# A list-scheduled attention and two-FFN kernel: longer transfer reserves in its planner, a wait narrowed to one PSUM bank, and a third token tile transposed by TensorE

## The chip, the cores and the metric

One core of one Trainium2 chip runs the whole program in one launch. The metric is device time in microseconds, the median of several runs. A difference under 0.3% (2 us here) can't be told from no change.

## The reference

For 4 sequences of 576 tokens, 8 heads of width 64, a windowed causal attention (64 keys back) is followed by two feed-forward layers over all 2304 tokens:

```python
scores = where((rel >= 0) & (rel < 64), q @ k.T / 8, -1e9)
x = softmax(scores) @ v                    # 2304 x 512
h = relu(x @ w_in); x = (h * h) @ w_out    # 512 -> 2048 -> 512
h = x @ w2_in                              # 512 -> 1024
solu = h * softmax(h)
out = layernorm(solu) * g_ln @ w2_out      # 1024 -> 512
```

## The kernel before

Each float32 product is made of three products (`TERMS`) of operands that were split into a high and a low part in a 32-bit matmul type. ScalarE (ACT) rounds the high part, VectorE (DVE) subtracts for the low one.

The order of all work is set before the program is built. Every piece is a task of `Plan`: an engine, a length in us, a rank, the tasks it comes after, buffer slots it takes and gives, and `late`, a time added behind its end before others may start. For a DMA `late` stands for the transfer, and the length for issuing it on SP's queue. `Plan.run` repeatedly starts the task that can start first (ties by rank), and the instructions are emitted in the order of the planned starts. On the chip each engine runs its own list in order and waits for the true dependencies by semaphores; nothing is reordered there. So a number in the plan changes no instruction, only its place.

Stages, in the order of time:

- **Stage one** (to about 140 us). Attention units of two 64-token blocks, 18 in all, run beside the first FFN for the first tokens (products of 256 and 512 columns: lines L693 for FFN1's first matmul, L709 for its second). A unit is: load q, k (`load_qk`) and v, scores on PE (L423), a mask and a maximum on DVE (L426, L431), exponentials on ACT (L448), a normalization (L458), a transpose, the product with v (`values`, L516 or L519), and for later tokens a store to DRAM (`store_x`). In the first ten units PE transposes (L476). PE fills its first 48 us with idle-time matmuls (`ps_warm`).
- **Stage two** (140 to about 257 us). The first FFN for the next 768 tokens, in eight rounds (`pair1`, t = 2) of seven half-size products each, 384 columns (L919), with the second matmul's products (L1036) between them. The last eight units run beside it. They are "crossed": DVE transposes 32x32 blocks (L482, `d`), a DMA writes them to DRAM (`aside`, L485), four DMAs read them back across partitions (`across`, L490, `pt`), and only then PE may run `values` (L516).
- **Stage three** (to about 434 us): the same FFN for the last 1024 tokens, 512 columns.
- **Stage four** (`pair2`, from about 434 us): the second FFN, nine pairs of 128-token tiles. A pair has seven products of six matmuls (L1314), in the order p1, p6, p7, p5, p2, p4, p3, into four banks a, b, d, c, of 512 columns: p1 and p2 go to a, p6 to b, p7 and p4 to d, p5 and p3 to c. `keep1` (ACT, L1320) copies p1 out of a; `u2`, `u3`, `c22`, `c21`, `c12` (DVE) and `c11` (ACT) add and copy banks. Then `behind` does softmax and layernorm for each tile: L1387 to L1406. The tile must be transposed for the last matmul (`mm_o`, L1455, 24 matmuls a tile). For the first 16 tiles DVE transposes blocks (L1415) and two DMA steps turn them through DRAM (L1418, L1424); for the last two (`TURNED`) PE transposes them, 8 matmuls each (L1438, `ps_lt`). `scaled` (ACT, L1460) and a store end a tile.

Of the kernel before, what the change touches and what calls it, by code (L numbers as in the profile page):

```python
# [20 lines left out]
P = 128  # L21
# [77 lines left out]
def kernel(  # L99
# [20 lines left out]
    NT, DM = out.shape  # L120
    DC = DM // P
    KF = w_in.shape[0]
# [6 lines left out]
    PASSES = [8, 0, 12, 16]  # L129
# [62 lines left out]
    with ExitStack() as c1:  # L192
# [7 lines left out]
        pass_of, starts = {}, []  # L200
# [8 lines left out]
        add = plan.add  # L209
# [134 lines left out]
        def attention(n, rank, after=()):  # L344
# [196 lines left out]
            if n == 0:  # L541
                lqs = [add("SP", 1.1, rank - 6, lambda h=h: load_qk(h), take=qk * (h == 0), late=2.0, at=0.7) for h in range(2)]
            else:
                lqs = [add("SP", 2.1 if alone else 2.2, rank - 6, lambda: load_qk(0), take=qk, late=2.0, at=0.7)]
            lv = add("SP", 0.9 if alone else 1.5, rank + (V0 if alone else -2), load_v, [v_after.get(n - 1) if n != 1 else None, *after], take=[vs], late=2.0, at=0.7)
            v_after[n] = lv
# [44 lines left out]
            else:  # L591
# [6 lines left out]
                if crossed:  # L598
                    c = add("DVE", 1.2, rank, blocks, ns, take=["raw"], give=["e"], port=True)
                    c = add("SP", 0.8, rank, aside, [c], late=LATE_P, give=["raw"])  # L600
                    c = [add("SP", 1.6, rank, across, [c, before], take=["pt"], late=LATE_P)]
                else:
                    c = [add("ACT", 0.48, rank, lambda a=a: copied(a), [p[a]], give=["a" if begins else "t"]) for a in range(2)]
                p = add("PE", 1.15, rank, lambda: values(0), [*c, lv], take=["t"], give=["pt", vs])
                if t < 2:
                    h = add("ACT", 0.48, rank, lambda: high(0), [p])
                    x_ready[n] = add("DVE", 0.60, rank, lambda: rest(0), [h], give=["t"])
                else:
                    h = add("ACT", 0.48, rank, taken, [p], take=["wm"], give=["t"])
                    x_ready[n] = add("SP", 0.8, rank, store_x, [h], late=2.8, give=["wm"])  # L610
            p_after[n] = p
# [72 lines left out]
        def ffn(n0, n1, kk, rank, done):  # L684
# [29 lines left out]
            if kk >= PUT:  # L714
# [10 lines left out]
                return  # L725
            r = add("ACT", N / 1200 + 0.11, rank, relu, [i], take=["r"], give=["a"])
            e = squares_of(o, N, rank, [r], signed=False)
# [167 lines left out]
        def pair1(t, j, at, unit, held, begins_after=()):  # L895
            N = HN[t]
# [3 lines left out]
            def rank(k):  # L900
                return at + unit * k
# [54 lines left out]
            def store(x, kk):  # L956
                nc.sync.dma_start(out=r_dram[t][kk], in_=o[x])
# [36 lines left out]
            for x, kk, f, k in (("c22", 2 * j + 1, f22, 6), ("u3", 2 * j, f21, 7)):  # L994
                f = squared(Named({}, o, x), N, rank(k) + 3, [f], False, True)
                r_ready[t, kk] = add("SP", 0.8, rank(k) + 3, lambda x=x, kk=kk: store(x, kk), [f], late=2.2, give=["wm"])

# [112 lines left out]
        PAIR0, PAIR = 10.88, 8.6  # L1110
        LATE, LATE_X, LATE_P, TOPS = 2.8, 4.0, 3.2, KF
        JOIN, SECOND, MORE = 4, 0.17, PASSES[1]
        SKIP = 6 if MORE else KF
# [40 lines left out]
        for t in (2, 3):  # L1154
# [13 lines left out]
            if t == 2:  # L1168
                lo, hi = begin[2] + 4, begin[3] - ENDS
                for i in range(PASSES[3] // 2):  # L1170
                    attention(starts[3] // 2 + i, lo + i * (hi - lo) / (PASSES[3] // 2), [xop[2, x][0] for x in ("S1", "S3", "S2", "S4")] if i < 2 else [])
                for m in range(NH2 * DC):
# [85 lines left out]
        def pair2(n, rank, rank_o):  # L1258
# [85 lines left out]
            def c12():  # L1344
# [3 lines left out]
            a = add("SP", 1.6, lead - 6, load_x, [x for _, t, at in tiles for x in stored[t, at * BLK // HN[t]]] + phase_of.get(n - 2, []) + [first_of[LAST, KF // 2 - 1] if n == 0 else past[LAST][-1], ready["2o", KF2 - 1] if n else None],  # L1348
                    take=["raw"], late=2.2)
            s1 = add("DVE", 0.72, lead, s13, [a], take=["raw"], port=True)  # L1350
# [9 lines left out]
            soon = rank - 30  # L1360
            free = read_of.get(n - 1, [])
            p1 = pe(0, "a", "A11", "B11", True, free if n > 1 else [], take=["a"] if n < 2 else ["b"] * (n == 2))
            e1 = add("ACT", 0.60, soon, keep1, [p1, *gone_by, *free])
            p6 = pe(1, "b", "S2", "T2", True, [p1, *free], take=["b"] * (n == 0))
            e2 = add("DVE", 0.68, soon, u2, [p6, e1, *gone_by, *free])
            p7 = pe(2, "d", "S3", "T3", True, [p6, *free], take=["a"] * (n < 2))
            p5 = pe(3, "c", "S1", "T1", True, [p7])
            e3 = add("DVE", 0.68, soon, u3, [p7, e2], take=["wm"])
# [6 lines left out]
            f12 = add("DVE", 0.68, soon, c12, [p3, f11, f21])  # L1375
            phase_of[n], read_of[n] = [p3], [f11, f12, f21]

# [3 lines left out]
        def behind(k, i, p, rank, rank_o, done):  # L1381
# [29 lines left out]

            by_pe = i >= NT // P - TURNED

# [59 lines left out]
            else:  # L1473
                p_ = add("DVE", 1.2, rank, blocks2, [a], port=True)
                r = add("ACT", 1.25, rank + 3, squares, [p_])
                p_ = add("SP", 0.8, rank, aside, [p_], late=2.4, give=["wb"])
                p_ = add("SP", 1.6, rank, across, [p_], take=["g"], late=2.4)
                r = add("POOL", 2.0, rank, root, [r], give=["wb"])
# [10 lines left out]

        EARLY0, LATE0, TURNED = 20, 20, 2  # L1490
        l_free = {(k, hf): past[LAST] for k in range(2) for hf in range(2)}
# [64 lines left out]
```

## Time and profile before

| | us |
|---|---|
| median of 3 runs | 651.33 (650.02 to 651.84) |
| the profiled execution | 651.62 |
| its span, first to last instruction | 649.8 |
| PE busy | 635.9 |
| DVE busy | 501.3 |
| ACT busy | 385.8 |
| POOL busy | 130.9 |

The span and busy times are of one profiled execution; its own time has 1.8 us around the span. PE's busy time includes overlap of pipelined matmuls, so it tells where PE is idle, not how close it is to its peak. L numbers are lines of the kernel before.

### The profile page before, as it was taken

To read this page: it belongs to the slowest core of one execution; us is meant where nothing else is said; L and a number is where in the kernel's file an instruction comes from. 1 tells how busy PE (TensorE), PEld (TensorE's weight loads), DVE (VectorE), ACT (ScalarE), POOL (GpSimd) and SP (SyncE) were. 2 spreads that over 40 slices of the span, in tenths; PEclk is the share of its full clock that TensorE was granted. 3 is DMA by queue.
4 is the path that set the end of the run, shared out by engine and by line. 5 is a ranking of instruction groups with operands and counts; after the bars stand their busy time and mean duration, and the time that the engine had idled before them with its cause. 6 is when DMAs were issued, how large, how long until landed. Compare 5 with 4: busy or idle time off the path is not lost.

```text
span 649.8 us, 11333 instructions
## 1 busy us (share of the span) xinstructions
PE 635.9 (98%) x4089; PEld 536.6 (83%) x4089; DVE 501.3 (77%) x872; ACT 385.8 (59%) x879; POOL 130.9 (20%) x164
## 2 busy tenths in 40 slices
PE   8999999999899999999999999999999999999997
PEld 4788877888889999998888888888887878878886
DVE  6998999599999663398887774499787798788761
ACT  5757757457767644466564554564755667557662
POOL 1012103123445433003333333100100110011000
PEclk9999999999999999999999999999999999999999
DMA  8887777215789667735431115742524643565311
GB/s 283 276 286 256 256 261 249 90 46 174 229 266 313 193 219 224 262 131 195 148 128 65 66 65 162 250 132 74 205 104 113 195 138 115 137 195 161 116 48 65
DMA packets 71353, 111.90 MB, mean 172 GB/s; under 512 B 6400, under 2 KB 42752, under 8 KB 71296
## 3 DMA queue, kind: packets, MB, share of 16 engines
q1 hardware_dynamic: 70752, 110.90, 52.5%
q8 instruction: 32, 0.52, 0.3%
q10 hardware_dynamic: 544, 0.26, 0.1%
q14 instruction: 25, 0.20, 0.1%
HBM read 76.01 MB, written 35.13 MB: 171 GB/s over the span
## 4 chain that ended last, share of the span: by engine, by line
PE 62%; DVE 5%; DMA 4%; ACT 3%; SPq 2%; issue 1%; ACTq 0%; DVEq 0%
PE ps_y L1036 22%; PE ps_h L919 17%; PE ps_o L1455 12%; PE ps_h L1314 10%; DMA l<-t_dram 1%; PE ps_v L516 1%; DMA pt<-p_dram 1%; SPq L1424 1%; DVE e L1398 1%; DMA p_dram<-d 1%; ACT o L1460 1%; ACT e L1406 1%; ACT e L448 1%; DVE wo L872 1%; DVE lnT L1448 1%
## 5 line engine op out<-in xcount | busy, mean ns | idle before, releaser
L1036 PE MATMUL ps_y<-g,wb 128*128 128x384 f32 (+1 forms) x768 | 163.7, 362 | 0.7 <-DVE g L642 0.7
L1036 PEld LDWEIGHTS ps_y<-g,wb 128*128 128x128 f32 x768 | 138.8, 188 | 16.7 <-DVE g L642 1.1
L1455 PE MATMUL ps_o<-w2o,lnT 128*128 128x512 f32 x432 | 100.4, 390 | 0.2 <-DVE lnT L1448 0.2
L1455 PEld LDWEIGHTS ps_o<-w2o,lnT 128*128 128x128 f32 x432 | 80.7, 188 | 17.8 <-DVE lnT L1448 0.5
L627 POOL TENSOR_TENSOR r<-r 128x512 f32<-128x512 f32 (+2 forms) x36 | 39.0, 1086 | 194.6 <-ACT r L699 116.8
L642 DVE TENSOR_TENSOR g<-r,g 128x512 fp32r<-128x512 f32 (+2 forms) x68 | 42.6, 627 | 28.1 <-ACT g L639 27.5
L627 POOL TENSOR_TENSOR u<-u 128x384 f32<-128x384 f32 (+1 forms) x48 | 47.9, 1003 | 77.9 <-ACT u L624 45.3
L1314 PE MATMUL ps_h<-w2i,xx 128*128 128x512 f32 x243 | 62.6, 390 | 0.0
L639 ACT ACTIVATE g<-r 128x512 fp32r<-128x512 f32 (+2 forms) x68 | 38.3, 566 | 33.7 <-PE ps_y L1036 16.9
L1314 PEld LDWEIGHTS ps_h<-w2i,xx 128*128 128x128 f32 x243 | 45.5, 188 | 9.8 <-DVE u L1324 0.3
L919 PE MATMUL ps_h<-xa,wo 128*128 128x512 f32 (+1 forms) x192 | 51.6, 368 | 0.0
L448 ACT ACTIVATE e<-e,nmax 128x128 f32<-128x128 f32 x112 | 43.5, 392 | 11.0 <-DVE nmax L431 10.9
L919 PE MATMUL ps_h<-xb,wo 128*128 128x384 f32 (+1 forms) x192 | 49.8, 358 | 0.0
L709 PE MATMUL ps_y<-g,wb 128*128 128x512 f32 (+1 forms) x240 | 48.3, 352 | 0.0
L693 PE MATMUL ps_h<-x,wa 128*128 128x512 f32 (+1 forms) x240 | 48.2, 352 | 0.1
L919 PE MATMUL ps_h<-xo,wo 128*128 128x512 f32 (+1 forms) x128 | 47.2, 369 | 0.0
L1409 POOL TENSOR_SCALAR rstd<-rstd 128x1 f32<-128x1 f32 x18 | 5.5, 307 | 203.3 <-ACT e L1406 185.2
L624 ACT ACTIVATE u<-u 128x384 f32<-128x384 f32 (+1 forms) x48 | 27.4, 576 | 29.5 <-DVE u L954 10.1
L693 PEld LDWEIGHTS ps_h<-x,wa 128*128 128x128 f32 x240 | 38.4, 189 | 7.3 <-issue 0.7
L709 PEld LDWEIGHTS ps_y<-g,wb 128*128 128x128 f32 x240 | 38.6, 189 | 6.1 <-issue 0.3
L919 PEld LDWEIGHTS ps_h<-xa,wo 128*128 128x128 f32 x192 | 35.2, 188 | 4.7 <-ACT wo L869 0.2
L1314 PE MATMUL ps_h<-w2x,xx 128*128 128x512 f32 x135 | 36.8, 392 | 1.8 <-ACT p L1320 1.8
(153 smaller groups left out, 1151.4 us busy)
## 6 DMA issues: line engine op xcount, KB each, us to landing
wraw<-in_w_in SPq DMA_DIRECT2D x24, 511.8 KB, 5.1
wraw<-in_w_out SPq DMA_DIRECT2D x24, 511.8 KB, 4.6
vt<-in_v SPq DMA_DIRECT2D x32, 256.0 KB, 3.5
t_dram<-h SPq DMA_DIRECT2D x16, 512.0 KB, 2.7
l<-t_dram SPq DMA_DIRECT2D x64, 128.0 KB, 3.7
kt<-in_k SPq DMA_DIRECT2D x16, 384.0 KB, 4.8
xr<-x_dram SPq DMA_DIRECT2D x18, 256.0 KB, 4.2
out<-o SPq DMA_DIRECT2D x18, 256.0 KB, 2.7
```

Source lines behind the costliest of these rows:

```text
L448: S.activation(out=o["er"][:, a, w], in_=s, func=AF.Exp, scale=SCALE if begins else 1.0, bias=o["nmax"][:, a, w : w + 1], accum_out=o["sum ...
L516: T.matmul(to.rearrange("p (a j) -> p a j", a=2), vt[:, i, h * BLK : h * BLK + BLK], pt[:, 2 * i : 2 * i + 2, par * HP + hp], start=True, ...
L624: S.activation(out=o["r"], in_=o["r"], func=AF.Relu)
L627: G.tensor_tensor(out=o["r"], in0=o["r"], in1=o["r"], op=ALU.mult)
L639: S.activation(out=o["g"][:, 0, :N], in_=o["r"], func=AF.Copy)
L642: V.tensor_tensor(out=o["g"][:, 1, :N], in0=o["r"], in1=o["g"][:, 0, :N].bitcast(F32), op=ALU.subtract)
L693: T.matmul(ps[:, :N], wa[kk][:, wi, c * P : c * P + P], xs[t][:, xi, c, n0:n1], start=n == 0, stop=n == 3 * DC - 1)
L709: T.matmul(acc[t, 0][d][:, n0:n1], wb[kk][:, wi, d * P : d * P + P], o["g"][:, xi, :N], start=kk == 0 and n == 0 and n0 == 0, stop=last an ...
L919: T.matmul(to[:, :N], w["t"][:, wi, off + c * P : off + c * P + P], (lo if xi else hi)()[:, c], start=begins and m == 0, stop=m == 5, skip ...
L1036: T.matmul(acc[t, half][d][:, :N], wb[kk][:, wi, d * P : d * P + P], q["g"][:, xi, :N], start=pos == 0 and n == 0, stop=pos == KF - 1 and ...
L1314: T.matmul(o[bank], o["xx", k][:, xi, at : at + P], w2i[w, r][wi][0](), start=begins and m == 0, stop=m == 5, skip_group_check=True)
L1455: T.matmul(o["o"], o["l", hf][:, xi, kk % 4, :], w2o[kk][:, wi, :], start=kk == 0 and n == 0, stop=kk == KF2 - 1 and n == 2)
```

## The change

1. The reserves `late` of several DMAs grow: attention's q and k from 2.0 to 3.2, v from 2.0 to 3.0, `across` from 3.2 to 4.6, `store_x` from 2.8 to 3.6 (the first four units keep 2.0 for q, k and v), one store of stage two's FFN from 2.2 to 3.4, stage four's read-back from 2.4 to 4.0 and its token load from 2.2 to 3.4.
2. In stage two, units after the second may not start before the FFN round two before has begun (`first_of[2, i - 1]`).
3. In stage four the planned order ties each product to the copy of its own bank in the pair before, where before p1, p6 and p7 were tied to three copies (`f11`, `f12`, `f21`) together.
4. Tiles 14, 16 and 17 are transposed by PE; before, 16 and 17.
5. Two of the last rounds' relu in stage one get an earlier rank.

```diff
-                lqs = [add("SP", 2.1 if alone else 2.2, rank - 6, lambda: load_qk(0), take=qk, late=2.0, at=0.7)]
+                lqs = [add("SP", 2.1 if alone else 2.2, rank - 6, lambda: load_qk(0), take=qk, late=2.0 if begins else LATE_Q, at=0.7)]
...
-                    c = [add("SP", 1.6, rank, across, [c, before], take=["pt"], late=LATE_P)]
+                    c = [add("SP", 1.6, rank, across, [c, before], take=["pt"], late=LATE_A)]
...
-            r = add("ACT", N / 1200 + 0.11, rank, relu, [i], take=["r"], give=["a"])
+            r = add("ACT", N / 1200 + 0.11, rank - 10 * (kk > KF - 3), relu, [i], take=["r"], give=["a"])
...
+        LATE_Q, LATE_V, LATE_A, LATE_S, LATE_R, LATE_T, LATE_L = 3.2, 3.0, 4.6, 3.6, 3.4, 4.0, 3.4
...
-                    attention(starts[3] // 2 + i, lo + i * (hi - lo) / (PASSES[3] // 2), [xop[2, x][0] for x in ("S1", "S3", "S2", "S4")] if i < 2 else [])
+                    attention(starts[3] // 2 + i, lo + i * (hi - lo) / (PASSES[3] // 2), [xop[2, x][0] for x in ("S1", "S3", "S2", "S4")] if i < 2 else [first_of[2, i - 1]])
...
-            free = read_of.get(n - 1, [])
-            p1 = pe(0, "a", "A11", "B11", True, free if n > 1 else [], take=["a"] if n < 2 else ["b"] * (n == 2))
-            e1 = add("ACT", 0.60, soon, keep1, [p1, *gone_by, *free])
-            p6 = pe(1, "b", "S2", "T2", True, [p1, *free], take=["b"] * (n == 0))
...
-            p7 = pe(2, "d", "S3", "T3", True, [p6, *free], take=["a"] * (n < 2))
-            p5 = pe(3, "c", "S1", "T1", True, [p7])
+            free = read_of.get(n - 1, {})
+            p1 = pe(0, "a", "A11", "B11", True, free.get("a", []) if n > 1 else [], take=["a"] if n < 2 else ["b"] * (n == 2))
+            e1 = add("ACT", 0.60, soon, keep1, [p1, *gone_by, *free.get("b", [])])
+            p6 = pe(1, "b", "S2", "T2", True, [p1, *free.get("b", [])], take=["b"] * (n == 0))
...
+            p7 = pe(2, "d", "S3", "T3", True, [p6, *free.get("d", [])], take=["a"] * (n < 2))
+            p5 = pe(3, "c", "S1", "T1", True, [p7, *free.get("c", [])])
...
-            phase_of[n], read_of[n] = [p3], [f11, f12, f21]
+            phase_of[n], read_of[n] = [p3], {"a": [f11], "b": [e2], "c": [f12], "d": [f21]}
...
-            by_pe = i >= NT // P - TURNED
+            by_pe = i in TURNED
...
-        EARLY0, LATE0, TURNED = 20, 20, 2
+        EARLY0, LATE0 = 20, 20
+        LASTS = NT // P
+        TURNED = (LASTS - 4, LASTS - 2, LASTS - 1)
```

PE's list in stage four, from the last product p3 of the sixth pair (rows of L1314: bank names 5435 and 5029 stand for the pairs a, d and c, b). Before:

```order
L1314 MATMUL ps_h_5029<-w2i,xx 128x512 x6
L1455 MATMUL ps_o<-w2o,lnT 128x512 x48
L1314 MATMUL ps_h_5435<-w2i,xx 128x512 x3
L1314 MATMUL ps_h_5435<-w2x,xx 128x512 x3
L1314 MATMUL ps_h_5029<-w2x,xx 128x512 x3
L1314 MATMUL ps_h_5029<-w2i,xx 128x512 x3
L1314 MATMUL ps_h_5435<-w2x,xx 128x512 x3
```

The same place now, where lines have moved by one:

```order
L1315 MATMUL ps_h_5029<-w2i,xx 128x512 x6
L1315 MATMUL ps_h_5435<-w2i,xx 128x512 x3
L1315 MATMUL ps_h_5435<-w2x,xx 128x512 x3
L1315 MATMUL ps_h_5029<-w2x,xx 128x512 x3
L1315 MATMUL ps_h_5029<-w2i,xx 128x512 x3
L1456 MATMUL ps_o<-w2o,lnT 128x512 x48
L1315 MATMUL ps_h_5435<-w2x,xx 128x512 x3
```

The next pair's p1 and p6 (twelve matmuls) now stand ahead of the 48 output matmuls, and its p7 behind them. This holds for the last four of the nine pairs; at the last one the eight transposes of tile 14 stand between the 48 and p7.

PE's list at the start of stage two, up to the scores of the first crossed unit (L423) and the next row. Before:

```order
L919 MATMUL ps_h_1947<-xb,wo 128x384 x6
L919 MATMUL ps_h_1946<-xb,wo 128x384
L919 MATMUL ps_h_1946<-xo,wo 128x384
L919 MATMUL ps_h_1946<-xb,wo 128x384 x2
L919 MATMUL ps_h_1946<-xo,wo 128x384
L919 MATMUL ps_h_1946<-xb,wo 128x384
L423 MATMUL ps_s<-kt,qt 64x128 x16
L919 MATMUL ps_h_1947<-xb,wo 128x384 x6
L919 MATMUL ps_h_1946<-xa,wo 128x384 x6
L709 MATMUL ps_y<-g,wb 128x512 x12
```

And now:

```order
L919 MATMUL ps_h_1929<-xb,wo 128x384 x6
L709 MATMUL ps_y<-g,wb 128x512 x12
L919 MATMUL ps_h_1928<-xb,wo 128x384
L919 MATMUL ps_h_1928<-xo,wo 128x384
L919 MATMUL ps_h_1928<-xb,wo 128x384 x2
L919 MATMUL ps_h_1928<-xo,wo 128x384
L919 MATMUL ps_h_1928<-xb,wo 128x384
L709 MATMUL ps_y<-g,wb 128x512 x12
L423 MATMUL ps_s<-kt,qt 64x128 x16
```

The twelve matmuls of L709 that stood behind the scores now stand ahead of them.

DVE's list from the mask of that unit (L426) to its maximum (L431). Before:

```order
L426 SCALAR_TENSOR_TENSOR e<-ps_s,mask 128x512
L947 TENSOR_TENSOR u_2045<-ps_h_1946,u_2029 128x384
L865 TENSOR_TENSOR ws<-w_472,ws 128x256
L872 TENSOR_TENSOR wo<-ws,wo 128x512
L872 TENSOR_TENSOR wz<-w_472,wz 128x256
L872 TENSOR_TENSOR wo<-ws,wo 128x512
L642 TENSOR_TENSOR g<-r,g 128x384
L431 TENSOR_REDUCE nmax<-e 128x4
```

And now:

```order
L674 COPY y<-ps_y 128x512
L642 TENSOR_TENSOR g<-r,g 128x384
L426 SCALAR_TENSOR_TENSOR e<-ps_s,mask 128x512
L939 TENSOR_TENSOR u_2056<-ps_h_1929,u_1963 128x384
L431 TENSOR_REDUCE nmax<-e 128x4
```

Six instructions stood between mask and maximum, one stands there now, and more of DVE's other work stands ahead of the mask.

## Rows read from the trace of the kernel before

**Rows 1.** Page, part 1: engine, busy us, share of span, instructions.
```profile
PE 635.9 (98%) x4089; PEld 536.6 (83%) x4089; DVE 501.3 (77%) x872; ACT 385.8 (59%) x879; POOL 130.9 (20%) x164
```

**Rows 2.** Windows by stage: stretch, length, then each engine's busy us, clock, DMA.
```profile
48.00:140.00 92.00, 90.84 (x725) 75.38 (x724) 79.45 (x134) 59.37 (x161) 16.53 (x15) 1.00 0.60 199
140.00:257.00 117.00, 112.72 (x1036) 105.27 (x1036) 94.98 (x168) 73.18 (x227) 48.50 (x50) 1.00 0.71 222
257.00:434.00 177.00, 177.00 (x829) 152.14 (x829) 125.07 (x191) 97.84 (x169) 43.41 (x47) 1.00 0.44 149
434.00:650.00 216.00, 210.13 (x928) 171.85 (x926) 161.85 (x287) 125.37 (x208) 16.26 (x36) 1.00 0.41 128
```

**Rows 3.** Waits of PE: who waits, for whom: us in all, times, longest.
```profile
PE ps_s L423 <- DMA kt<-in_k: 1.8, 2, 1.0
PE ps_h L1314 <- ACT p L1320: 1.8, 2, 1.1
...
PE ps_v L516 <- DVE nmax L431: 0.7, 1, 0.7
PE ps_h L919 <- DVE u L950: 0.7, 1, 0.7
PE ps_y L1036 <- DVE g L642: 0.7, 1, 0.7
PE ps_v L516 <- DMA pt<-p_dram: 0.6, 1, 0.6
```

**Rows 4.** Timeline of PE near 150 us: start, us, instruction, idle before.
```profile
150.12 1.21 PE L919 MATMUL ps_h<-xa,wz 128*128 128x384 f32 x6
152.06 0.45 PE L919 MATMUL ps_h<-xc,wo 128*128 128x384 f32 x1 [0.73 <-DVE u L950]
```

**Rows 5.** Chain of work, in order of time: start, us, what.
```profile
194.94 1.04 PE ps_y L1036 x6
...
517.65 10.89 PE ps_o L1455 x48
...
630.53 0.87 PE ps_lt L1438 x8
```

**Rows 6.** Timeline of ACT and PE, 526 to 533 us.
```profile
527.47 1.16 ACT L1402 ACTIVATE e<-e,nmu 128x1024 f32<-128x1024 f32 x1 [0.62 <-DVE nmu L1399]
...
528.53 0.67 ACT L1460 ACTIVATE o<-ps_o,rstd 128x512 f32<-128x512 f32 x1
...
531.75 0.58 ACT L1320 ACTIVATE p<-ps_h 128x512 f32<-128x512 f32 x1
...
532.38 0.96 PE L1314 MATMUL ps_h<-w2x,xx 128*128 128x512 f32 x3 [1.13 <-ACT p L1320]
```

**Rows 7.** DMA issues: out<-in, times, KB each, median us to landing.
```profile
kt<-in_k SPq DMA_DIRECT2D x16, 384.0 KB, 4.8
...
pt<-p_dram SPq DMA_DIRECT2D x32, 128.0 KB, 4.4
```

**Rows 8.** Timeline of all engines, 43 to 57 us, cut to PE and DVE rows.
```profile
43.72 1.10 PE L423 MATMUL ps_s<-kt,qt 64*64 64x128 f32 x32
...
45.74 1.28 DVE L458 TENSOR_TENSOR e<-e,sums 128x512 f32<-128x512 f32 x2
...
54.51 2.12 DVE L458 TENSOR_TENSOR e<-e,sums 128x512 f32<-128x512 f32 x2
...
56.51 0.71 PE L476 MATMUL ps_p<-ident,e 128*128 128x128 f32 x5
```

**Rows 9.** Timeline, first crossed unit: scores, mask, maximum, product with v.
```profile
143.07 1.10 PE L423 MATMUL ps_s<-kt,qt 64*64 64x128 f32 x32
...
146.83 0.68 DVE L426 SCALAR_TENSOR_TENSOR e<-ps_s,mask 128x512 f32<-128x512 f32 x1
...
150.87 0.68 DVE L431 TENSOR_REDUCE nmax<-e 128x4 f32<-128x512 f32 x1
...
172.67 1.15 PE L516 MATMUL ps_v<-pt,vt 128*64 128x64 f32 x32
```

More of the change, by code (lines that the diff above doesn't have):

```diff
@@ L543, in attention @@
             else:
-                lqs = [add("SP", 2.1 if alone else 2.2, rank - 6, lambda: load_qk(0), take=qk, late=2.0, at=0.7)]
-            lv = add("SP", 0.9 if alone else 1.5, rank + (V0 if alone else -2), load_v, [v_after.get(n - 1) if n != 1 else None, *after], take=[vs], late=2.0, at=0.7)
+                lqs = [add("SP", 2.1 if alone else 2.2, rank - 6, lambda: load_qk(0), take=qk, late=2.0 if begins else LATE_Q, at=0.7)]
+            lv = add("SP", 0.9 if alone else 1.5, rank + (V0 if alone else -2), load_v, [v_after.get(n - 1) if n != 1 else None, *after], take=[vs], late=2.0 if begins else LATE_V, at=0.7)
             v_after[n] = lv
@@ L609, in attention @@
                     h = add("ACT", 0.48, rank, taken, [p], take=["wm"], give=["t"])
-                    x_ready[n] = add("SP", 0.8, rank, store_x, [h], late=2.8, give=["wm"])
+                    x_ready[n] = add("SP", 0.8, rank, store_x, [h], late=LATE_S, give=["wm"])
             p_after[n] = p
@@ L995, in pair1 @@
                 f = squared(Named({}, o, x), N, rank(k) + 3, [f], False, True)
-                r_ready[t, kk] = add("SP", 0.8, rank(k) + 3, lambda x=x, kk=kk: store(x, kk), [f], late=2.2, give=["wm"])
+                r_ready[t, kk] = add("SP", 0.8, rank(k) + 3, lambda x=x, kk=kk: store(x, kk), [f], late=LATE_R if t == 2 else 2.2, give=["wm"])
             for x, kk, f, slot, k, seconds in (("c11", 2 * j, f11, "r", 3, (10, 11) if lastj else (10, 13)), ("c12", 2 * j + 1, f12, "wm", 9, (12, 13) if lastj else (16, 19))):
@@ L1348, in pair2 @@
             a = add("SP", 1.6, lead - 6, load_x, [x for _, t, at in tiles for x in stored[t, at * BLK // HN[t]]] + phase_of.get(n - 2, []) + [first_of[LAST, KF // 2 - 1] if n == 0 else past[LAST][-1], ready["2o", KF2 - 1] if n else None],
-                    take=["raw"], late=2.2)
+                    take=["raw"], late=LATE_L)
             s1 = add("DVE", 0.72, lead, s13, [a], take=["raw"], port=True)
@@ L1360, in pair2 @@
             soon = rank - 30
-            free = read_of.get(n - 1, [])
-            p1 = pe(0, "a", "A11", "B11", True, free if n > 1 else [], take=["a"] if n < 2 else ["b"] * (n == 2))
-            e1 = add("ACT", 0.60, soon, keep1, [p1, *gone_by, *free])
-            p6 = pe(1, "b", "S2", "T2", True, [p1, *free], take=["b"] * (n == 0))
-            e2 = add("DVE", 0.68, soon, u2, [p6, e1, *gone_by, *free])
-            p7 = pe(2, "d", "S3", "T3", True, [p6, *free], take=["a"] * (n < 2))
-            p5 = pe(3, "c", "S1", "T1", True, [p7])
+            free = read_of.get(n - 1, {})
+            p1 = pe(0, "a", "A11", "B11", True, free.get("a", []) if n > 1 else [], take=["a"] if n < 2 else ["b"] * (n == 2))
+            e1 = add("ACT", 0.60, soon, keep1, [p1, *gone_by, *free.get("b", [])])
+            p6 = pe(1, "b", "S2", "T2", True, [p1, *free.get("b", [])], take=["b"] * (n == 0))
+            e2 = add("DVE", 0.68, soon, u2, [p6, e1, *gone_by, *free.get("c", [])])
+            p7 = pe(2, "d", "S3", "T3", True, [p6, *free.get("d", [])], take=["a"] * (n < 2))
+            p5 = pe(3, "c", "S1", "T1", True, [p7, *free.get("c", [])])
             e3 = add("DVE", 0.68, soon, u3, [p7, e2], take=["wm"])
@@ L1476, in behind @@
                 p_ = add("SP", 0.8, rank, aside, [p_], late=2.4, give=["wb"])
-                p_ = add("SP", 1.6, rank, across, [p_], take=["g"], late=2.4)
+                p_ = add("SP", 1.6, rank, across, [p_], take=["g"], late=LATE_T)
                 r = add("POOL", 2.0, rank, root, [r], give=["wb"])
```

## The prediction

> **What bounds the kernel now.** I read the page first: PE is busy 98% of the span, DVE 77%, ACT 59% [rows 1]. So a change is worth what it takes from or adds to PE's idle time and PE's work, and nothing else. The windows by stage show where PE is idle: 1.2 us between 48 and 140 us, 4.3 us in stage two, none in stage three, 5.9 us in stage four [rows 2] (the last of which holds the store behind PE's last product). In the first 48 us idle-time matmuls fill the gaps, and their number stays. The granted clock is 1.00 of full speed in every window, its higher level, so the clock has no term here.
>
> The waits of PE name the idle time [rows 3]: 1.8 us in two waits for a transfer of kt (at 71 us and, of the same size, at 166 us), 1.8 us in two waits of p7 for the copy `keep1`, and in stage two four waits of 0.6 to 0.7 us. A wait costs a little more than its listed idle. An example: six products start at 150.12, the next one at 152.06, so 1.94 us for work that takes 1.04 us elsewhere; 0.90 us is lost, 0.73 us is listed [rows 4, 5]. I add 0.17 us to each wait.
>
> The sum is made against the profiled execution's 651.62 us, which is 0.3 us above the median of the three runs; its span is 649.8 us, with 1.8 us around it that I leave.
>
> **The tail: waits for one bank's copy.** Before, p1 and p6 of the next pair stand behind the 48 output matmuls, so p7 follows `keep1`'s source directly. The chain shows the 48 as 10.89 us of work [rows 5]. Bank d cannot be given to p7 before `keep1` has emptied bank a of p1: the timeline has `keep1` from 531.75 to 532.33, and p7 at 532.38 after an idle 1.13 us [rows 6]. Now, for the last four pairs, the 48 stand between p6 and p7. `keep1` gets 10.89 us of cover for what took under 2 us. So the second of the two waits, in the sixth pair's successor (0.7 + 0.17), goes. The first one belongs to a pair whose product order is not changed; but on ACT one `scaled`, 0.67 us long [rows 6], now stands earlier, so that `keep1` starts some 0.6 us sooner. It falls from 1.1 + 0.17 to about 0.7. Together 2.1 us become 0.7: **-1.4**. Upper bound of the gain 2.1 (both gone), lower 0.8 (the first unchanged). What is late next: p7's own operands and p1's. The bank p1 wants is freed by `c11`, which stands ahead of the copies it waited for before, and the operands of the next pair are rounded about 3.5 us ahead of p1's new place by the order of before. I price this at nothing. If that cover were gone, p1 would wait for a rounding on ACT, about one instruction of 0.6 us, four times.
>
> Tile 14's eight transposes are new PE work. The same operation on tile 16 or 17 takes 0.87 us for eight on PE [rows 5]: **+0.9**. They stand behind 48 output matmuls, so tile 14's normalization has 10.89 + 2.7 us of cover for about 7 us of chain. Their copies out of PSUM go to ACT and DVE, which are not the bound. The two DMA steps that fall away for that tile hid behind PE work already, so they give nothing.
>
> A rule speaks against this. The Trainium skill, page "TensorE: Matmul & The Clock Gate", section "Part 4: PE-mode transpose", puts a full 128x128 transpose at about 275 ns within a kernel and says that its output lands in PSUM and wants a copy. By it, eight would be an estimated 2.2 us, and the sum would come out 1.3 us higher than by the row. The row has 0.87 us for eight.
>
> **Longer reserves for kt.** The loads land 4.8 us after issue at the median [rows 7], and the planner reserved 2.0. With 3.2 the planner puts scores later behind their load; in the new order the scores at both places stand further behind it. I let both kt waits go: 1.8 + 2 x 0.17, **-2.1**. Bounds: 0 (the load is still later than its reserve) to -2.1.
>
> **Stage two.** The other four waits are worth 0.7 + 0.7 + 0.7 + 0.6 [rows 3] and 4 x 0.17: 3.4 us. One is for DVE's u, one for DVE's g, two for a crossed unit's probabilities coming back from DRAM. New places: units start one by one over the whole stage, not crowded in its first half. So DVE and ACT have less to do at once, and I let all four go: **-3.4**.
>
> But the same table moves scores and `values` of a unit against each other. Between them lie mask, maximum, exponentials, normalization, transpose, p_dram, pt: the DVE-to-DRAM round trip. With PE work at the rates of the rows (384-column products 0.173 us apiece, from 1.04 us for six; 32 scores or 32 small products about 1.1 to 1.2 us [rows 9]; 12 of 512 columns 2.72 us, a quarter of the 10.89) the order gives this cover. First unit: before 78 + 30 products of 384, twelve of 512 and four score blocks, 26.3 us without waits; now the twelve of 512 stand ahead of its scores, 23.6 us. Second: 27.6 (26.8 before). Last: 28.4 (40.9 before). The rest have 29.6 or more. What is needed: the first unit's scores began at 143.07 and its `values` at 172.67, which is 29.6 us with no wait at its end [rows 9], so 29.6 is an upper bound. In it the maximum started 4.0 us after the mask, and six other DVE instructions stood between. Now one does, which takes about 3.4 us out of the chain: 26.2 us. Against 23.6 of cover that is a wait of up to 2.6; I take **+2.0**, since the 29.6 held some slack. The other crossed units I give together **+1.0**, one wait of the size seen before. Stage two is then -3.4 + 3.0 = -0.4. Bounds: -3.4 (no new wait) to +5.8 (the 29.6 us hold for each unit, worked out below).
>
> Queued behind a waiting `values` on PE is everything: the first FFN's products, for which ACT and DVE then wait. On SP's queue three reads of r now stand between the writing of p_dram and the four reads pt (4.4 us to landing [rows 7]); each costs an issue, well under 1 us together, and is inside the range.
>
> **Stage one.** Six units there have their scores later. The tightest is the one whose scores began at 43.72 and whose transposes at 56.51, a cover of 12.8 us; normalization ended at 54.51 + 2.12 = 56.63 [rows 8], so there was no slack. In the new order some 10.4 us of PE work lie there. The same two normalization instructions took 1.28 us ten microseconds earlier [rows 8], and its mask started two microseconds late behind other DVE work. With the load spread, most of the 2.4 us comes back: **+0.5**, bounds 0 to 2.4. The earlier relu is ACT work with ACT 59% busy: nothing; a wait for one would be one relu, about 0.4 us.
>
> **The sum.** -1.4 + 0.9 - 2.1 - 0.4 + 0.5 = -2.5. From 651.62 that is 649.1 for a profiled execution, and 648.8 against the median of 651.33.
>
> **The rivals.**
>
> *All named waits vanish and nothing new comes.* Then -1.4 - 2.1 - 3.4 + 0.9 = -6.0: **645.3**. For it: the waits are real and each has a cause that the new order addresses, and DVE, busy 94.98 of 117 us in stage two [rows 2], gets room. Against it: the shorter cover of the first, second and last unit.
>
> *Stages one and two give back what they gain.* kt's transfer or a unit's round trip is simply late somewhere else; only the tail is left: -1.4 + 0.9 = -0.5, **650.8**, no change that can be told. For it: PE is busy 112.72 of 117 us in stage two [rows 2], and the waits there are small ones of four different causes, which tend to move. Against it: the reserves are nearer to 4.8 and 4.4 us than before.
>
> *The DRAM round trip decides, and it is slower.* If a crossed unit needs the 29.6 us seen, covers of 23.6, 27.6 and 28.4 leave waits of 6.0, 2.0 and 1.2, 9.2 us in place of 3.0: 6.2 more than my sum, **655.0** against the median. It is slower than before from a round trip of about 28.5 us on (waits of 4.9 and 0.9, and the last unit's at nothing, with stage one at its 2.4 bound). For it: the row of 29.6 itself. Against it: the six instructions between mask and maximum are gone, and `values` there waited for nothing.
>
> *The transposes wait for their copies.* The eight write PSUM, and p7 of the last pair stands directly behind them. If PE has to wait twice for a copy out of that bank, of the size of the 0.67 us that an eviction takes in [rows 6], the time is 1.3 higher than my sum: **650.1**. The profile would show a stretch of over 2 us there. The row speaks against it with 0.87 us for the eight of tile 16 or 17 and no idle time behind them [rows 5]. The page of the Trainium skill named above asks for such a copy, and its figure gives about the same 1.3.
>
> **How the numbers follow.** Forecast 0.49, all gone 0.20, given back 0.18, round trip 0.11, transposes 0.02. The likeliest is mine: **648.8**, its own range 647.2 to 650.4 (kt one wait not gone, +1.1; first unit 0.6 more; or 1.6 less where the first unit's wait is small). The bound of a difference is 0.3%, 2 us: below 649.4 is faster, above 653.3 slower. About two thirds of my own case lie below 649.4: 0.33, with the 0.20 makes faster 0.53. Same: 0.16 + 0.18 + 0.02 = 0.36. Slower: 0.11. The range takes in the all-gone case and half of the slower one: 645.0 to 652.5.
>
> **What the profile of the changed kernel would show.** Right: no wait of p7 for `keep1` above 0.7 us and only one; 24 transposes of L1438 (moved by one line) in three groups of about 0.87 us; p7 behind 48 output matmuls without idle; no row of PE waiting for kt; stage two near 116.5 us of length with one wait of about 2 us at the first crossed unit's `values`. Wrong: that wait at 5 us or more, or one at the last unit (round trip); scores still waiting for kt; a new wait of p1 for ACT's rounding in stage four; stage one longer by over 1 us with PE waiting for a normalization. What would make the prediction wrong above all is a round trip longer than 27 us, and on the other side an order in which the waits of stage two do not come back at all.

## The result and the profile after

The changed kernel takes 654.98 us (median of 5 runs, 654.13 to 655.58) against 651.33 us (650.02 to 652.20 in 5 runs beside it): ratio 1.0056, interval 1.004 to 1.0072. It is slower by some 3.7 us. The forecast was 648.8 us, with 655.0 us for the rival in which a crossed unit's way through DRAM decides. The time is that of the rival; the reason isn't, as the rows show.

Part 1 of the page of the kernel after, and its windows by stage, to be held against [rows 1] and [rows 2]:

```profile
PE 640.3 (98%) x4097; PEld 537.7 (82%) x4097; DVE 500.0 (77%) x871; ACT 386.7 (59%) x879; POOL 129.9 (20%) x164
```
```profile
48.00:140.00 92.00, 91.92 (x756) 76.58 (x756) 80.79 (x138) 60.53 (x168) 15.89 (x15) 1.00 0.63 208
140.00:257.00 117.00, 112.10 (x1002) 103.77 (x1001) 95.74 (x168) 72.88 (x226) 47.95 (x50) 1.00 0.67 212
257.00:434.00 177.00, 176.08 (x848) 151.28 (x849) 122.98 (x187) 96.47 (x166) 42.97 (x47) 1.00 0.45 153
```

PE's idle time between 48 and 140 us is 0.1 us instead of 1.2. Stage two has 4.9 us instead of 4.3, and stage three, which had none, has 0.9. So up to there nothing is won and little lost. The list of PE's waits shows that the names have changed (compare [rows 3]):

```profile
PE ps_y L1036 <- DVE g L642: 1.3, 3, 0.6
...
PE ps_h L919 <- DVE wo L872: 1.0, 1, 1.0
PE ps_h L919 <- DVE u L947: 0.9, 1, 0.9
PE ps_h L1315 <- DVE h L1346: 0.8, 4, 0.2
PE ps_s L423 <- DMA kt<-in_k: 0.8, 1, 0.8
PE ps_y L1036 <- ACT g L639: 0.7, 1, 0.7
PE ps_h L919 <- ACT r L943: 0.6, 1, 0.6
PE ps_h L919 <- DVE u L954: 0.5, 1, 0.5
```

No row has L1315 waiting for `keep1`, and none has `values` (L516) waiting for pt. One wait for kt, 0.8 us, is still there. The rows that answer to [rows 9], from the timelines of PE and DVE (first crossed unit: scores, mask, maximum, product with v; the fourth row is the second crossed unit's scores):

```profile
145.07 1.10 PE L423 MATMUL ps_s<-kt,qt 64*64 64x128 f32 x32
...
146.84 0.68 DVE L426 SCALAR_TENSOR_TENSOR e<-ps_s,mask 128x512 f32<-128x512 f32 x1
...
147.94 0.68 DVE L431 TENSOR_REDUCE nmax<-e 128x4 f32<-128x512 f32 x1
...
152.34 1.22 PE L423 MATMUL ps_s<-kt,qt 64*64 64x128 f32 x32 [0.76 <-DMA kt<-in_k]
...
172.07 1.15 PE L516 MATMUL ps_v<-pt,vt 128*64 128x64 f32 x31
```

27.0 us lie between scores and `values`, with no wait at their end; the forecast put a 2.0 us wait there, the rival 6.0. PE itself waited three times in between, 2.1 us (0.76 for kt, 1.00 for wo, 0.33 for g), which gave the unit so much more time. The way through DRAM does not decide.

Stage four does. From the start of its first product to the start of its last there are 185.0 us, 440.8 to 625.8; before, from 439.1 to 622.0, 182.9 us. From the summary of the line, the kernel after first, then the kernel before, then the kernel `early_alone` of the first experiment:

```profile
L1315 PE MATMUL ps_h<-w2i,xx x243: 387/389/501, 440.8 to 625.8; 128*128 128x512 f32 x122
```
```profile
L1314 PE MATMUL ps_h<-w2i,xx x243: 387/389/501, 439.1 to 622.0; 128*128 128x512 f32 x122
```
```profile
L1315 PE MATMUL ps_h<-w2i,xx x243: 388/389/499, 439.1 to 620.9; 128*128 128x512 f32 x122
```

What happens at one of the four places where p1 and p6 now stand ahead of the 48 output matmuls, from the timeline of all engines of the kernel after (L1337 is `c11`, L1343 `c21`, L1346 `c12`; PEld is a product's weight load):

```profile
560.23 0.60 ACT L1337 ACTIVATE h<-ps_h 128x512 f32<-128x512 f32 x1 [3.65 <-PE ps_h L1315]
...
560.86 0.69 DVE L1343 TENSOR_TENSOR h<-ps_h,u 128x512 f32<-128x512 f32 x1 [2.06 <-ACT h L1337]
...
561.60 0.53 PEld L1315 LDWEIGHTS ps_h<-w2i,xx 128*128 128x128 f32 x3 [0.48 <-DVE h L1343]
...
562.72 0.68 DVE L1346 TENSOR_TENSOR h<-ps_h,u 128x512 f32<-128x512 f32 x1
...
563.46 0.53 PEld L1315 LDWEIGHTS ps_h<-w2x,xx 128*128 128x128 f32 x3 [0.62 <-DVE h L1346]
563.46 0.96 PE L1315 MATMUL ps_h<-w2x,xx 128*128 128x512 f32 x3 [0.19 <-DVE h L1346]
```

Read it upwards. p6 (last two rows) writes bank b, which `u2` emptied long ago. Yet it starts when `c12` ends, and `c12` reads bank c. p1 writes bank a, which `c11` has left at 560.83, yet its weights load when `c21`, a reader of d, ends. And `c21` itself starts when `c11` ends, though both only read, from different banks. In the code, from the third pair on, a and d are the halves of one tile of two banks; c and b are those of another. The waits follow the tile. So the planned order was tied to the own bank's copy, and the program was not. From the starts of the products in the trace, p1 loses 0.22 + 0.11 us and p6 0.36 + 0.11, the second number the slower restart behind it: 0.8 us at each of four places, 3.2 us in all. The list of waits shows a quarter of it. One wait of p7 for `keep1` is left, too short for that list: in the pair whose order did not change, p7's weights load behind `keep1` (L1321), and p7 starts 0.25 us late and runs 0.13 us longer.

```profile
532.54 0.58 ACT L1321 ACTIVATE p<-ps_h 128x512 f32<-128x512 f32 x1
...
533.17 0.53 PEld L1315 LDWEIGHTS ps_h<-w2x,xx 128*128 128x128 f32 x3 [0.52 <-ACT p L1321]
```

Eight transposes of tile 14 are there, with no wait around them (618.36, the next product 619.15): 0.8 us.

### The profile page after: what moved, and what is told of

The parts are those of the page before. It is cut to its first block, busy times and chain, and to the rows that moved or that the text cites. A ratio compares the mean times of both kernels' runs of the same rounds, so it can differ in the third digit from the quotient of the medians.

```text
span 653.6 us, 11324 instructions
## 1 busy us (share of the span) xinstructions
PE 640.3 (98%) x4097; PEld 537.7 (82%) x4097; DVE 500.0 (77%) x871; ACT 386.7 (59%) x879; POOL 129.9 (20%) x164
## 4 chain that ended last, share of the span: by engine, by line
PE 76%; DVE 12%; DMA 4%; ACT 2%; issue 2%; SPq 2%; POOL 0%; DVEq 0%; ACTq 0%; POOLq 0%
PE ps_y L1036 20%; PE ps_h L919 17%; PE ps_o L1456 10%; PE ps_h L1315 8%; PE ps_y L709 7%; PE ps_h L693 7%; PE ps_s L423 2%; DMA xr<-x_dram 2%; PE ps_v L516 1%; PE ps_v L519 1%; DVE e L1399 1%; DVE wo L872 1%; DVE g L642 1%; SPq L1425 1%; PE ps_p L476 1%
## 5 line engine op out<-in xcount | busy, mean ns | idle before, releaser
L627 POOL TENSOR_TENSOR r<-r 128x512 f32<-128x512 f32 (+2 forms) x36 | 37.5, 1042 | 207.0 <-ACT r L699 106.6
L1315 PE MATMUL ps_h<-w2i,xx 128*128 128x512 f32 x243 | 63.2, 392 | 0.2
L627 POOL TENSOR_TENSOR u<-u 128x384 f32<-128x384 f32 (+1 forms) x48 | 49.4, 1035 | 59.1 <-ACT u L624 42.3
L1315 PEld LDWEIGHTS ps_h<-w2i,xx 128*128 128x128 f32 x243 | 45.1, 188 | 11.7 <-DVE h L1343 1.9
L709 PE MATMUL ps_y<-g,wb 128*128 128x512 f32 (+1 forms) x240 | 48.7, 353 | 0.1
L709 PEld LDWEIGHTS ps_y<-g,wb 128*128 128x128 f32 x240 | 38.6, 189 | 6.4 <-DVE g L642 0.5
L1315 PE MATMUL ps_h<-w2x,xx 128*128 128x512 f32 x135 | 37.9, 395 | 0.9 <-DVE h L1346 0.8
```

What stands on the lines that cost most here:

```text
L627: G.tensor_tensor(out=o["r"], in0=o["r"], in1=o["r"], op=ALU.mult)
L709: T.matmul(acc[t, 0][d][:, n0:n1], wb[kk][:, wi, d * P : d * P + P], o["g"][:, xi, :N], start=kk == 0 and n == 0 and n0 == 0, stop=last an ...
L1315: T.matmul(o[bank], o["xx", k][:, xi, at : at + P], w2i[w, r][wi][0](), start=begins and m == 0, stop=m == 5, skip_group_check=True)
```

## The experiments

The kernels were timed in groups, on several chips. A ratio is always to runs of the kernel before in the same group (medians 651.1 to 652.2 us); where two kernels are compared that were not in one group, this is said.

**Which half.** The change falls into two kernels: the edits of stages one and two on the old stage four (`early_alone`), and those of stage four on the old stages one and two (`tail_alone`). PE's list up to stage four is that of the changed kernel in the one, that of before in the other.

```diff
 tail_alone: parts 3 and 4 of the change, and of its part 1
-                    take=["raw"], late=2.2)
+                    take=["raw"], late=LATE_L)
-                p_ = add("SP", 1.6, rank, across, [p_], take=["g"], late=2.4)
+                p_ = add("SP", 1.6, rank, across, [p_], take=["g"], late=LATE_T)
 early_alone: parts 2 and 5, and the rest of part 1
```

> Only the edits of stage four (each product tied to its own bank's copy, the longer reserves of that stage, tile 14 turned by TensorE); stages one to three stand as before. Theory T, the new tail costs time by itself: the trace after the change has 3.2 us of new waits there (in each of four pairs p1 waits 0.2 for c21 and p6 0.4 for c12, each with 0.1 of restart), 0.87 us of transposes, and about 2.1 us of old waits gone; about 653.3 us, 2.0 above before. Rival, the forecast's own sum for the tail (-1.4 + 0.9) was right and the new waits there only follow from what came earlier: about 650.8 us, and no wait of p6 for c12.

> Only the edits of stages one and two (longer reserves of attention's loads, of the read-back and of the stores, units tied to the rounds, the earlier relu); stage four stands as before. Theory T, two separate losses: the old waits of stage two go but 8.0 us of others stand in their place, 2.5 us more than before, and stage one with the start gives back 0.8; about 653.0 us, 1.7 above before. Rival, the whole loss is of the tail: about 651 us or less. Rival, the whole loss is of stage two: about 655 us.

Measured: tail alone 655.41 us, ratio 1.0045 (1.0027 to 1.0063); early alone 651.54 us, ratio 0.9995 (0.998 to 1.0011). The loss is that of stage four: theory T's 1.7 us for stages one and two was a miss, and its rival (the whole loss is of the tail) came true. The trace of the early half shows stage four's products from 439.1 to 620.9 us, 181.8 us (row above), so the new stage four costs 3.2 us more than the old one behind the same stages.

The runs tell a second thing. Before spread from 649.5 to 655.0 us over 35 runs on this chip, the tail alone from 653.1 to 657.9, the early half only from 650.6 to 652.2. The longest wait for kt in four traces of the old order is 1.0, 2.2, 2.3 and 2.5 us, and none shows in the early half's list; in six other traces of the new stages with the tie the longest is 0.3 to 0.8 us. After one of these waits the granted clock fell; windows of the kernel `before_split`, below:

```profile
160.00:165.00 5.00, 5.00 (x55) 4.58 (x55) 4.37 (x9) 3.27 (x14) 3.89 (x4) 1.00 0.50 173
165.00:170.00 5.00, 2.71 (x30) 2.42 (x32) 5.00 (x10) 4.70 (x20) 1.34 (x2) 1.00 1.03 300
170.00:175.00 5.00, 5.00 (x43) 4.73 (x34) 3.96 (x8) 2.29 (x7) 2.92 (x4) 0.66 0.54 188
```

PE idles 2.3 us of the middle window, and in the next one its clock is 0.66 on average, between its two levels. One trace of before, with a wait of 1.0 us, showed none of this. The runs agree with it without proving it: of the 35 runs of before, 14 had a granted clock below 0.999 over the whole run, and their median is 653.2 us against 651.0 for the rest; of the early half's twelve none had.

**One tile for each bank.** The decisive one: the same order of work, with single-bank tiles from the third pair on.

```diff
-                elif begins and bank not in o:
-                    if n in (0, 2):
-                        kept.append(ps_b.tile([P, 2, 512], F32, tag="b", name="ps_h2"))
+                elif begins and n < 2 and bank not in o:
...
+                elif begins and bank not in o:
+                    if not singles:
+                        c2.close()
+                        ps_s = c1.enter_context(tc.tile_pool(name="ps_s", bufs=1, space=PSUM))
+                        singles.update((x, ps_s.tile([P, 512], F32, tag=x, name="ps_h2" + x)) for x in "abcd")
+                    o.update(singles)
```

> The kernel of the first run of this call, with the four banks a, b, c, d as four tiles of one bank each from the third pair on, in place of two tiles of two banks. Theory T (a product waits for every reader of its whole tile, so p1 waits for the copy of bank d and p6 for the copy of bank c): p1 and p6 no longer wait, 3.2 us less than with two-bank tiles, about 650.1 us. Rival (the copies are simply late, or reading beside a product that writes is slow): no change against the two-bank tiles, about 653.3 us.

> The kernel before, with the banks a, b, c, d as four tiles of one bank each from the third pair on; its order is the same. Theory T (the wait of p7, which writes bank d, for keep1, which reads bank a, is there only since both are one tile): both waits of p7 for keep1 go, 1.3 + 0.8 us, and a smaller one of 0.15; about 649.1 us. Rival (p7 needs keep1 for another reason, or the split costs a wait where the two-bank tiles are given back): 651.3 us or more.

> The changed kernel with the banks a, b, c, d of stage four as four tiles of one bank each; its order is the same. Theory T (the tail's loss is that products wait for all readers of a two-bank tile): what the split took from the trace of the tail alone, 4.5 us, goes here too: about 650.5 us. Rival (the tail's waits are covered by something else once stages one and two are the new ones): above 653 us.

> The new stages one and two with the old order of stage four, and four one-bank tiles. Theory T: the trace of the early edits alone has 2.8 us of waits in stage four, and the split takes all but nothing of them: 651.5 - 2.7, about 648.8 us, and the runs lie as close together as those of the early edits alone (1.6 us), since it has the same loads. Rival (the split's gain is a draw of the old stages' loads, which vary): 651.5 us.

Measured: tail with the split 649.65 us, ratio 0.9969 (0.995 to 0.9988), 5.8 us under the tail with two-bank tiles; before with the split 649.65 us, 0.9967 (0.9948 to 0.9985); after with the split 650.60 us, 0.997 (0.9954 to 0.9987), 4.4 under the changed kernel (not in one group; against the runs of before beside each, 5.2); early with the split 649.68 us, 0.9966 (0.9947 to 0.9984). All four are nearer to theory T than to its rival. The traces put the gain into stage four: its products take 180.5 us in `after_split` in place of 185.0, 180.5 in `tail_split` for 184.9, 179.5 in `before_split` for 182.9, 179.5 in `early_split` for 181.8. The same place as above, in the trace of `after_split` (now L1342 is `c11`, L1348 `c21`, L1351 `c12`):

```profile
556.22 0.84 PE L1320 MATMUL ps_h2d<-w2x,xx 128*128 128x512 f32 x3
556.41 0.60 ACT L1342 ACTIVATE h<-ps_h2a 128x512 f32<-128x512 f32 x1 [2.29 <-PE ps_h2a L1320]
...
557.77 0.69 DVE L1348 TENSOR_TENSOR h<-ps_h2d,u 128x512 f32<-128x512 f32 x1 [1.43 <-PE ps_h2d L1320]
...
558.94 0.84 PE L1320 MATMUL ps_h2a<-w2i,xx 128*128 128x512 f32 x3
...
559.64 0.68 DVE L1351 TENSOR_TENSOR h<-ps_h2c,u 128x512 f32<-128x512 f32 x1
...
560.30 0.84 PE L1320 MATMUL ps_h2b<-w2x,xx 128*128 128x512 f32 x3
```

`c11` now reads bank a from 556.41 to 557.01 while p4 (first row) already writes bank d, and p6 (last row) stands straight behind p1, without a wait for `c12`. No row of L1320 is left in the list of waits. Of the 4.5 us, the four places make 3.2 to 3.4; the rest are the small wait for `keep1` (0.4) and one of the output matmuls for lnT (0.22 listed, 0.6 lost). In `before_split` the two waits of p7 for `keep1` [rows 3, 6] are gone too: they were of the same kind. So with one tile for each bank there is nothing left for the new order to gain: the new stage four then takes 1.0 us more than the old one by the traces (180.5 against 179.5) and 0.9 by the medians (650.60 against 649.68, in one group), about the price of the eight transposes. The Trainium skill, page "PSUM — Partial Sum Buffer", section "PSUM bank collisions raise a hardware error", says that two engines, readers included, must not be at one bank in the same 32 partitions at once, and that work on different banks runs clean. By that rule, a guard for each bank is enough, and the trace agrees: `c11` and p4 lie side by side.

**The tie to the own bank's copy, and tile 14.** Each undone by itself in the changed kernel, whose own runs are of another group.

```diff
 after_three_copies
-            phase_of[n], read_of[n] = [p3], {"a": [f11], "b": [e2], "c": [f12], "d": [f21]}
+            phase_of[n], read_of[n] = [p3], {x: [f11, f12, f21] for x in "abd"}
 after_unturned
-        TURNED = (LASTS - 4, LASTS - 2, LASTS - 1)
+        TURNED = (LASTS - 2, LASTS - 1)
```

> The changed kernel with p1, p6 and p7 tied to three copies (c11, c12, c21) of the pair before in the planned order again; all else as changed. In the order the 48 output matmuls then stand between p1 and p6 at two of the four places and ahead of p1 at the other two, as before. Theory T (p6 has to wait for c12 wherever it stands straight behind p1 and p3): p6's four waits of 0.36 + 0.11 go, p1's stay at two places, and one or two waits of p7 for keep1 come back at 0.6 to 0.9: 1.8 less than the changed kernel, about 653.2 us. Rival (the tie to the own bank's copy costs nothing): 655 us.

> The changed kernel with tile 14 turned by DVE and two DMA steps again. Theory T (the eight transposes cost their 0.87 us on PE and nothing else): about 654.1 us. Rival (the way through DRAM would have come too late in the new order, so that the transposes pay for themselves): 655 us or more.

Measured: with three copies 654.98 us, ratio 1.0058 (1.0036 to 1.008): the rival, and a miss for theory T. p6's waits did go where the 48 stand between p1 and p6, but the 48 then wait. The timeline:

```profile
541.13 0.68 DVE L1346 TENSOR_TENSOR h<-ps_h,u 128x512 f32<-128x512 f32 x1
...
541.72 2.49 DVE L1449 TENSOR_TENSOR lnT<-l,lnT 128x512 fp32r<-128x512 f32 x4
...
542.46 1.88 PE L1456 MATMUL ps_o<-w2o,lnT 128*128 128x512 f32 x7 [0.56 <-DVE lnT L1449]
```

Their operand lnT stands behind `c12` on DVE's list, so the wait for `c12` has only another name.

Tile 14 unturned: 657.06 us, ratio 1.0083 (1.0054 to 1.0112), again the rival. Against the changed kernel the groups differ, and the two intervals overlap; the traces decide. Without the transposes stage four's products take 184.1 us, 0.9 less, but from the last product to the end there are 30.2 us in place of 27.8. DVE's half of tile 14's lnT (L1449) now stands behind `c12` of the last pair:

```profile
624.86 1.22 DVE L1388 TENSOR_REDUCE nmax<-h 128x1 f32<-128x1024 f32 x1
626.00 0.68 DVE L1346 TENSOR_TENSOR h<-ps_h,u 128x512 f32<-128x512 f32 x1
...
626.60 2.61 DVE L1449 TENSOR_TENSOR lnT<-l,lnT 128x512 fp32r<-128x512 f32 x4
...
627.33 3.02 PE L1456 MATMUL ps_o<-w2o,lnT 128*128 128x512 f32 x12 [2.15 <-DVE lnT L1449]
```

**Stages one and two.** Here the old waits went and others came for no net gain. Parts of the edits were tried one at a time, most with single-bank tiles and the old order of stage four:

```diff
 loads_alone (on the kernel before): late=2.0 -> 3.2 for q, k and 3.0 for v, all else as before
 tie_split (on before_split)
-                    attention(starts[3] // 2 + i, lo + i * (hi - lo) / (PASSES[3] // 2), [xop[2, x][0] for x in ("S1", "S3", "S2", "S4")] if i < 2 else [])
+                    attention(starts[3] // 2 + i, lo + i * (hi - lo) / (PASSES[3] // 2), [xop[2, x][0] for x in ("S1", "S3", "S2", "S4")] if i < 2 else [first_of[2, i - 1]])
 nofirst_split (on early_split), after_no_tie (on the changed kernel): the same line turned back
```

> The kernel before with the longer reserves of attention's q, k and v loads alone (3.2 and 3.0); stage four as before. Theory T (the old order's wait for kt, 1.0 us in one trace, 2.4 us in two others and there with a lower granted clock behind it in one, is what spreads the runs of the old stages over 5 us): no wait for kt above 1 us, runs within 2 us of each other, and a median at or below 651.5 us. Rival (the spread is of something else, or needs the tie to the rounds or the other reserves): runs spread over 4 us or more.

> The kernel before with the tie of units to rounds alone, and four one-bank tiles. Its counterpart without the tie has 649.7 us, runs from 647.6 to 652.4 us. Theory S (the tie takes the spread away): runs within 2.5 us, no lower granted clock, no wait for kt above 1 us, median about 649.5 us. Rival (the reserves do it, or the whole set): runs spread over 4 us.

> The new stages one and two without the tie of units to rounds, old order of stage four, four one-bank tiles. Its counterpart with the tie has 649.7 us, runs from 648.9 to 651.2 us. Theory S (the tie to the rounds is what keeps a unit's scores behind their load, so that it takes the spread away, and its price is DVE work late in stage two): runs spread over 4 us or more, with waits for kt of 2 us in some and a lower granted clock in some; median 650 us or above. Rival (the reserves do it): spread under 2.5 us, and a median at or under 649.7 us.

Measured: loads alone 653.44 us, ratio 1.0031 (1.0009 to 1.0052), runs from 652.2 to 658.0, with a granted clock as low as 0.995 over a run: not narrower than before on that chip (649.0 to 655.1), a miss, though its trace has a wait for kt of only 0.6 us. The tie alone 656.49 us, 1.0081 (1.0059 to 1.0104), some 6.8 us above its counterpart of another group. The whole set of early edits without the tie, `nofirst_split`, 648.88 us, 0.9966 (0.9953 to 0.998), runs from 647.9 to 649.4. So theory S fails: the tie by itself brings no gain, its six runs spread over 2.5 us with granted clocks down to 0.995, and these twelve runs are close together without it. Waits of PE in `tie_split`:

```profile
PE ps_v L517 <- DMA r_dram<-u: 2.2, 1, 2.2
PE ps_y L1037 <- ACT g L640: 1.7, 1, 1.7
PE ps_v L517 <- DMA pt<-p_dram: 1.6, 1, 1.6
PE ps_h L920 <- DVE u L940: 1.3, 1, 1.3
```

With the old reserves, `values` waits in a tied kernel: here the rival of the forecast happens, in another kernel. For the price of the tie in the new stages, three more runs on one chip:

> New stages one and two with the tie, old order of stage four, four one-bank tiles: 649.7 us before on another chip. Here about 649.5 us, as the reference of the next run.

> The same without the tie: 648.9 us on another chip. If the tie costs the 2.3 us that one trace shows less in stage two, 2.3 below the run before it; if the medians of the two chips tell it, 0.8 below; if it costs nothing, the same.

> The changed kernel without the tie of units to rounds; stage four as changed. If the tie costs 2.3 us: 652.7 us. If 0.8 us: 654.2 us. If the stage-two waits only move: 655 us.

Measured: 649.46 us with the tie, 647.11 without (ratio to before 0.9931, interval 0.9915 to 0.9947), and the changed kernel without the tie 652.92 (1.0029, 1.0015 to 1.0043), 2.1 under the changed one of another group. The tie costs some 2.4 us by the pair of one group; stage four starts 2.4 to 3.1 us earlier without it in all three pairs of traces. The pair `early_split` and `nofirst_split`, of two groups, differs by 0.8 us only. On the spread the runs do not agree: those of the changed kernel without the tie reach from 652.3 to 655.2 us, and the three slowest of the twelve have a granted clock of 0.997. So whether the tie narrows the spread stays open. Without it, these waits are left in the stretch, for `nofirst_split_again`:

```profile
PE ps_s L424 <- DMA kt<-in_k: 1.5, 1, 1.5
...
PE ps_h L920 <- ACT p L932: 0.7, 1, 0.7
...
PE ps_h L920 <- ACT r L944: 0.5, 1, 0.5
```

The four waits for g and those for u and wo are gone; the wait for kt is longer than with the tie (0.3). This kernel, with the new reserves, the earlier relu, single-bank tiles, no tie and the old order and turning of stage four, is the fastest of those timed here, 4.5 us under before on its chip.

## Why the prediction was wrong

- **What failed: "I price this at nothing."** The forecast asked what p1 needs in its new place, and looked at the copy of its own bank and at its operands; for p6 it did not ask. The waits that came are for the other bank of the same tile: p1 for `c21`, p6 for `c12`. Measured 3.2 us in the trace; the split, which takes all such waits away, gave 4.4 to 5.8 us. The step before it held the same fault: "Bank d cannot be given to p7 before `keep1` has emptied bank a" took the wait in [rows 6] for one that the banks ask for. The text ahead of the forecast has it as well, where it says that engines wait for "the true dependencies": in this program they wait for those of whole tiles. The forecast's -1.4 for the tail was right for what went (of the waits for `keep1` 0.4 us is left, 0.7 was forecast). But with the transposes the stage was to become 0.5 us shorter, and by the traces it became 2.0 us longer behind the old stages (`tail_alone`, 184.9 against 182.9) and 3.2 behind the new ones.
- **The transposes: size right, cover wrong.** 0.8 us measured, 0.9 forecast. But the way through DVE and DRAM that they replace was not hidden in the new order; against "so they give nothing" stands PE's wait of 2.15 us for tile 14's lnT without them.
- **Stages one to three: nothing in place of -2.0.** The terms were -2.1 for kt, -0.4 for stage two, +0.5 for stage one; `early_alone` stands at 651.54 against 651.5. Here the rival "stages one and two give back what they gain" was right.
- **Stage two: the old waits went, others came.** Its terms were -3.4 for old waits and +3.0 for late `values`. The old waits went, but no `values` is late. In their place PE waits eight times for results of DVE and ACT (u, g, wo and r), 5.0 us listed: five times in stage two, 3.3 us, and three times in stage three, 1.7 us, for which the forecast had no term. The argument that with units starting one by one "DVE and ACT have less to do at once" failed: some 2.4 us of it come from the tie that spreads them. That the first unit's chain gets shorter held: its maximum starts 1.1 us after the mask, where it was 4.0. The 27.0 us are only an upper bound for the chain, as 29.6 was before; the last read of pt was issued by 165.06, and reads of pt landed 4.4 to 5.0 us after issue, so that I estimate some 25 us, against the forecast's 26.2. (It put the issues of three reads "well under 1 us together"; issues on SP's queue take 0.3 to 0.4 us each in the traces, so three are an estimated 1.0 to 1.3.)
- **kt: half right, and the row was one draw.** -2.1 was for both waits, 0.8 and 1.0 us in one trace. In the trace after, the wait in stage one is gone; one of 0.8 us stands in stage two, at another unit. Other executions of the old order show 2.2 to 2.5 us for one wait. The whole set of early edits shortens it to 0.8 us or less in seven traces. This hardly moves the median, perhaps since the new waits cost about as much, and the runs lie closer together. The reserves of the loads alone do not do it; which of the others it takes was not tried.
- **Stage one: wrong sign, small.** +0.5 forecast; PE's idle time there fell from 1.2 to 0.1 us, most of it the kt wait.
- **The rival with the right time** asked for late `values` at 29.6 us. It needed a trace to tell that 655 us was not its proof.

Open: the tail alone is 3.9 us slower than before by the medians, where its trace shows stage four 2.0 us longer (438.3 to 623.2 us, 184.9 against 182.9). Part of that is the granted clock: 7 of its 12 runs had one below 0.999, of the runs of before 14 of 35. Between the runs at 0.999 or above the difference is 2.9 us (653.9 against 651.0). The rest wasn't settled.

## What to carry to other kernels

When a product moves in a list, ask what the program makes it wait for: not the bytes that it overwrites but every reader of the tile that they were allocated in. A wait in a trace that no data flow explains (`keep1` reading a, p7 writing d) is a hint at that, and to remove its cause is worth more than an order around it: the split alone, with no order changed, took 0.3% off the kernel before. Edits of a plan that leave the median where it was can still narrow the spread of the runs, so look at both; which of the edits did it here isn't known. A tie that spaces work out is to be timed by itself.

## What was not expected of the hardware

The same order of stages one to three had its longest wait for kt at 1.0, 2.2, 2.3 and 2.5 us in four executions (`before`, `tail_alone`, `before_split`, `tail_split`), so that a wait read from one trace is no fixed price. Behind 2.3 us without a product the granted clock was 0.66 over the next five microseconds in `before_split` (from 171 to 173 us it was 0.50, the lower level); behind 2.2 us in `tail_alone` and 2.5 us in `tail_split` it stayed at 1.00. The windows of `tail_alone`:

```profile
165.00:170.00 5.00, 2.80 (x43) 2.33 (x42) 5.00 (x9) 3.48 (x15) 0.83 (x1) 1.00 0.79 252
170.00:175.00 5.00, 5.00 (x55) 4.68 (x54) 4.94 (x10) 4.11 (x14) 2.82 (x3) 1.00 0.53 144
```
